# Windowed attention and a gated convolution block on one core: casts of w_out by transfers, and guards and clamps on another engine

## The chip, the core and the metric

One Trainium2 chip, of which the kernel uses one core. The metric is the device time of one execution in microseconds. The core has engines with a queue each: TensorE (PE in the profile; its weight loads are PEld), VectorE (DVE), ScalarE (ACT), GpSimd (POOL) and SyncE (SP), which here only issues transfers. Each queue is worked through in order: an instruction that waits holds up all that stands behind it.

## The reference, cut to what matters

```python
# 8 batches, 8 heads, 576 positions, 64 per head; window of 64 positions back
scores = scale * np.matmul(q, k.transpose(0, 1, 3, 2))
scores = np.where(mask, scores, -1000000000.0)        # 0 <= i - j < 64
attn = np.exp(scores - np.max(scores, axis=-1, keepdims=True))
attn = attn / (np.sum(attn, axis=-1, keepdims=True) + 1e-09)
x = heads_side_by_side(np.matmul(attn, v))            # (8, 576, 512)

h = np.maximum(x @ w_in, 0.0)                         # w_in 512 x 1024
conv_out = sum(conv_w[k] * shifted(h, k - 1) for k in range(3))   # along positions
gate = 1.0 / (1.0 + np.exp(-conv_out))
return (h * gate) @ w_out                             # w_out 1024 x 512
```

The weights come in as 64-bit floats, everything else in 32 bits.

## The kernel before, in words

The 8 x 576 positions are cut into 12 units of 384. For each unit the kernel computes attention and then the block with `w_in`, the convolution, the gate and `w_out`. Attention of later units runs while the matrix products of earlier ones do.

**Attention.** A unit is worked in three chunks `b`. `qk` (L350) makes scores, `row_max` (L357) adds the mask and takes the negative row maximum `nm`, `exps` (L367) takes exponents and their sums `sm`. `guard` (L370) adds 1e-9 to the sums, `reciprocal` (L373) inverts them into `r`, and `normalise` (L378) multiplies. For units 0 and 1 the result is transposed on TensorE (L384) and copied into `ub` by ScalarE (L389); later units use VectorE and 24 small transfers. For unit 2 GpSimd zeroes parts of `ub` (L411, L412). `values` (L481) multiplies with `v`. In the units 0, 1 and 2 `guard` is put on GpSimd, from unit 3 on it is on VectorE.

**Two halves.** The large products use float32r, a rounded type. So that precision isn't lost, each operand is split into a rounded high half and the rest: `xh` (ScalarE, L485) and `xl` (VectorE, L488), `wih` and `wil`, `woh` and `wol`, `gh` (ScalarE, L551) and `gl` (VectorE, L555). Each product is three matmuls, high by high, high by low and low by high: L501 for `w_in`, L564 for `w_out`.

**The block.** L522 is the ReLU into `hbuf`, L528 and L535 the convolution, L542 the sigmoid, L547 the gate.

**The weights.** The 64-bit words are loaded into `bits` (L264) and turned into float32 by integer and float operations in `to_f32`: an absolute value on ScalarE (L248), a clamp from below by 2^-15 on GpSimd (L249), a shift and mask (L250), sign and exponent (L252) on VectorE, a scaled copy of the low words on ScalarE (L255), and their sum on VectorE (L256). `weights` then casts the result `x` to the high half on GpSimd (L269) and subtracts it on VectorE for the low half (L270). `w_in` comes in five calls, parts (0), (1), (2, 3), (4, 5), (6, 7); `w_out` in four, (0, 1), (2, 3), (4, 5), (6, 7). A part has 512 columns, so a call handles 512 or 1024. There are two buffers of `bits` and two of `x`; the loads of a later call wait until L256 of an earlier one has read `bits`, and L248 of a later call waits until L270 has read `x`. The convolution's weights go through the same `to_f32`, with 24 columns.

**The order.** Every step is put on a list by `at` with a due time, an engine, a cost in microseconds, and what it reads and writes. `queued` then plays the list through: the engine that can start earliest takes the most urgent step that is ready, and the order so found is that of each engine's queue. It is found when the kernel is built. `two` marks a step that is taken to need the port that VectorE and GpSimd share. For a step that moves data, the plan takes it to end some time after its issue:

```python
if x.mb:
    dma = max(dma, start) + x.mb * 2.7
    end = dma + 1.9
```

Where TensorE would have nothing to do in the first 110 us of the plan, matmuls on a tile of zeros (`spare`, L212) are put in its queue.

Of the kernel before, what the change touches and what calls it, by code (L numbers as in the profile page):

```python
# [8 lines left out]
F32 = mybir.dt.float32  # L9
# [3 lines left out]
ALU = mybir.AluOpType  # L13
# [20 lines left out]
TINY = 2.0 ** -15  # L34
# [127 lines left out]
PORT_CL = 0.5  # L162
# [5 lines left out]
def attention_moe(ctx: ExitStack, tc: tile.TileContext, q, k, v, w_in, conv_w, w_out, out):  # L168
    nc = tc.nc
# [48 lines left out]
    def at(t, eng, cost, do, r=(), w=(), kind=None, mb=0, port=0.0):  # L218

        plan.append(Work(t, eng, cost, do, list(r), list(w), kind, mb, port))  # L220

    def two(t, eng, cost, do, **kw):
        at(t, eng, cost, do, port=cost, **kw)
# [17 lines left out]

    def to_f32(t, n, st, x, kb, kt):

        lw, hw, xu = st[..., 0], st[..., 1], x.bitcast(U32)

        at(t, "ACT", 0.0009 * n + 0.2, lambda: nc.scalar.activation(x, hw.bitcast(F32), AF.Abs), r=kb, w=kt)  # L248
        at(t, "POOL", 0.0027 * n + 0.02, lambda: nc.gpsimd.tensor_scalar(x, x, TINY, None, op0=ALU.max), w=kt, port=PORT_CL)  # L249
        two(t, "DVE", 0.00052 * n + 0.06, lambda: nc.vector.tensor_scalar(  # L250
            xu, xu, 3, 0x3FFFFFF8, op0=ALU.logical_shift_left, op1=ALU.bitwise_and), w=kt)
        two(t, "DVE", 0.00104 * n + 0.07, lambda: nc.vector.scalar_tensor_tensor(  # L252
            xu, hw, 0xC0000000, xu, op0=ALU.bitwise_and, op1=ALU.bitwise_or), r=kb, w=kt)

        at(t, "ACT", 0.0009 * n + 0.2, lambda: nc.scalar.activation(lw, lw, AF.Copy, scale=2.0 ** -29), w=kb)  # L255
        two(t, "DVE", 0.00104 * n + 0.07, lambda: nc.vector.tensor_tensor(xu, xu, lw, ALU.add), r=kb, w=kt)  # L256

    def weights(t, src, fs, hi, lo, key, buf, halves):

        e = slice(halves[0] * DM, (halves[-1] + 1) * DM)  # L260
        st, x = bits[buf][:, e], w24[buf][:, e]
        kb, kt = [("bits", buf, a) for a in halves], [("w24", buf, a) for a in halves]
        for f, a, tl in zip(fs, halves, load_at(buf, halves, t)):
            at(tl, "SP", 0.7, lambda f=f, a=a: nc.sync.dma_start(  # L264
                bits[buf][:, a * DM:(a + 1) * DM], src[f].bitcast(U32).rearrange("p (e two) -> p e two", two=2)),
               w=[("bits", buf, a)], mb=0.52)
        n = len(fs) * DM
        to_f32(t, n, st, x, kb, kt)
        two(t, "POOL", 0.00127 * n, lambda: nc.gpsimd.tensor_copy(hi, x), r=kt, w=[f"{key}{f}h" for f in fs])  # L269
        two(t, "DVE", 0.00104 * n + 0.07, lambda: nc.vector.tensor_tensor(lo, x, hi.bitcast(F32), ALU.subtract),  # L270
           r=kt + [f"{key}{f}h" for f in fs], w=[f"{key}{f}l" for f in fs])

    freed = {}

    def load_at(buf, halves, t):

        ts = [freed.get((buf, a), START["bits"][buf][a]) for a in halves]
        for a in halves:
            freed[(buf, a)] = t + 0.01
        return ts  # L280
# [20 lines left out]
    def wide(u):  # L301
        return u < BY_PE

    def place_of(b, i):

        return divmod(NB * b + i, NT)

    def block(u, b, i):

        first = (u * NT + place_of(b, i)[1]) % SB == 0  # L310
        return (P, W if first else 0, 0) if wide(u) else (KW, 0, 2 if first else 1)
# [25 lines left out]
    def bank_keys(u, b):  # L337
        return {1: [("po", 2), ("po", 3)], 2: [("po", 0), ("po", 1)]}.get(b, [("sc", 0)]) if u == 0 else [("sc", 0)]

    def qk(u, b):  # L340
        rows = W if wide(u) else HW
        for i in range(NB):
            g, t0 = place_of(b, i)
            n, o, _ = block(u, b, i)
            for p in range(2):
                for s in range(0, W, rows):
                    r, t = p * W + s, t0 * W + s
                    for h in range(2):
                        hs = slice(h * D, (h + 1) * D)
                        nc.tensor.matmul(banks_of(u, b)[h][r:r + rows, i * P + o:i * P + n], qs[hs, 2 * g + p, t:t + rows],  # L350
                                         ks[hs, 2 * g + p, t + o:t + n], start=True, stop=True)

    def row_max(u, b):
        for i in range(NB):
            n, o, m = block(u, b, i)
            for h in range(2):
                nc.vector.tensor_tensor_reduce(  # L357
                    out=ss[b][:, i, h, o:n], in0=banks_of(u, b)[h][:, i * P + o:i * P + n], in1=mask[m][:, o:n],
                    scale=-0.125, scalar=3.0e38, op0=ALU.add, op1=ALU.min,
                    accum_out=nms[b][:, 2 * i + h:2 * i + h + 1])  # L360

    def exps(u, b, i):
        n, o, _ = block(u, b, i)
        for h in range(2):
            e = slice(2 * i + h, 2 * i + h + 1)
            x = ss[b][:, i, h, o:n]
            nc.scalar.activation(x, x, AF.Exp, bias=nms[b][:, e], scale=-1.0, accum_out=sms[b][:, e])  # L367

    def guard(b, on):
        on.tensor_scalar_add(sms[b], sms[b], 1e-9)  # L370

    def reciprocal(b):
        nc.vector.reciprocal(rs[b], sms[b])  # L373

    def normalise(u, b, on):
        n = P if wide(u) else KW
        sv = ss[b].rearrange("p t h k -> p (t h) k")[:, :, :n]
        on.tensor_tensor(sv, sv, rs[b].unsqueeze(2).broadcast_to([P, 2 * NB, n]), ALU.mult)  # L378
# [40 lines left out]
    def needed(b):  # L419

        keys = []
        for i in range(NB):
            g, t = place_of(b, i)
            n = int(t >= (4, 2)[g])
            keys += [("q", g, n)] + [("k", g, j) for j in range(n + 1)]
        return list(dict.fromkeys(keys))

    def softmax(u, b, t, ex_at):
        at(t, "PE", 0.90 if wide(u) else 0.82, lambda b=b: qk(u, b), r=needed(b), w=bank_keys(u, b),
           kind="tiled" if wide(u) else "eight")  # L430
        for i in range(NB):
            if block(u, b, i)[1]:
                at(t + 0.1, "POOL", 0.2, lambda b=b, i=i: nc.gpsimd.memset(ss[b][:, i, :, :W], 0.0), w=[("s", b, i)])
        at(t + 0.002, "DVE", 1.69 if wide(u) else 1.45, lambda b=b: row_max(u, b),
           r=bank_keys(u, b) + (["mask0"] if wide(u) else ["mask1", "mask2"]), w=[("s", b, i) for i in range(NB)] + [("nm", b)])
        t = ex_at
        for i in range(NB):
            at(t, "ACT", 0.78 if wide(u) else 0.74, lambda b=b, i=i: exps(u, b, i), r=[("nm", b)],
               w=[("s", b, i), ("sm", b, i)], kind="exp")
        t += 0.45  # L440
        sw = [("sm", b, i) for i in range(NB)]
        if u < 3:
            at(t, "POOL", 0.6, lambda b=b: guard(b, nc.gpsimd), w=sw)
        else:
            at(t, "DVE", 0.15, lambda b=b: guard(b, nc.vector), w=sw)
        at(t, "DVE", 0.15, lambda b=b: reciprocal(b), r=sw, w=[("r", b)])
        sr = [("s", b, i) for i in range(NB)]
        if u < 3:
            two(t, "DVE", 1.15 if wide(u) else 0.88, lambda b=b: normalise(u, b, nc.vector), r=[("r", b)], w=sr)
        else:  # L450
            two(t, "POOL", 1.5, lambda b=b: normalise(u, b, nc.gpsimd), r=[("r", b)], w=sr)
        t += 0.4
        if u < BY_PE:
            for j in range(2):
                m, g = ("po", (2 * b + j) % NC), place_of(b, NB // 2 * j)[0]
                at(t, "PE", 0.66, lambda b=b, j=j: transpose_pe(b, j), r=sr + ["mask0"], w=[m])
                at(t + 0.1, "ACT", 0.55, lambda b=b, j=j: untile(b, j), r=[m], w=[("u", g, i) for i in range(4)])
            return
        t = max(t, when[-1][2] + 0.1)
        for g, t0, rows in parts(b):  # L460
            at(t, "DVE", 0.12 * 2 * len(rows), lambda b=b, g=g, t0=t0, rows=rows: transpose(b, g, t0, rows), r=sr,
               w=[("T", g)] + [("bits", i, a) for i in T_BITS[g] for a in range(2)])
            if t0 + len(rows) == NT:
                if u == BY_PE:
                    at(t + 0.01, "POOL", 1.0, lambda g=g: zero_blocks(g), w=[("u", g, i) for i in range(4)])
                for i in range(4):
                    at(t + 0.05, "SP", 2.1, lambda g=g, i=i: place(g, i), r=[("T", g)], w=[("u", g, i)], mb=0.15)
# [263 lines left out]
```

## Time and profile before

| | |
|---|---|
| median of 3 runs | 532.17 us (531.51 to 532.33) |
| the profiled execution | 531.34 us |
| its span in the profile | 529.6 us, 1.74 us less than the execution |
| busy, share of the span | PE 98%, PEld 94%, DVE 72%, ACT 72%, POOL 21% |
| granted clock of TensorE | 1.0 |
| GpSimd's clamps, L249 | 9 of `w` with 23.9 us, one of `cw` with 0.3 |
| GpSimd's casts, L269 | 5 of `w_in` with 5.7 us, 4 of `w_out` with 5.6 |
| GpSimd's guards, L370 | 9 with 7.2 us |
| transfers | all issued by SP; 39.7% of what 16 engines could do |

Rows of the profile's timeline give start and duration in us, the engine, the line, the operation, what it writes and reads, the shapes, and in brackets how long its engine had been idle and what ended that. Rows of its groups give count, busy time in us and the mean of one in ns, then the idle time in front of them.

### The profile page before, as it was taken

The page shows a single profiled execution, that of the slowest core. Times are in us where ns is not written, and L with a number is a line of the kernel's source. Part 1 is how long each engine was busy: PE and PEld are TensorE (multiplying, and loading weights), DVE is VectorE, ACT ScalarE, POOL GpSimd, SP SyncE. Part 2 cuts the span into 40 slices and gives each one's busy share as a digit, 9 for nine tenths or more (in the row PEclk, how much of TensorE's full clock was granted, in tenths as well). Part 3 has the DMA queues.
Part 4 walks back from the last instruction along what each step waited for, and adds up shares of the span by engine and source line. Part 5 has one row for each costly group of instructions (what it writes and reads, how often), then busy time and mean ns, then how long its engine had stood idle before and what let it go on. Part 6 is the DMA issues. An engine that isn't in the chain of part 4 may idle for free.

```text
span 529.6 us, 14836 instructions
## 1 busy us (share of the span) xinstructions
PE 518.5 (98%) x5826; PEld 499.8 (94%) x5826; DVE 380.3 (72%) x1084; ACT 379.7 (72%) x1011; POOL 112.6 (21%) x196
## 2 busy tenths in 40 slices
PE   9998999999999999999999999999999999999996
PEld 8887889999999999999999999999999999999996
DVE  3899999985858667767767767767767667655552
ACT  2997897579896696696697687687687687544542
POOL 6664467113131011021021021021021021000000
PEclk9999999999999999999999999999999999999999
DMA  8984660237292173183083074073073053010011
GB/s 284 365 296 136 208 231 1 60 109 248 76 325 72 58 256 83 42 291 77 21 297 77 16 253 122 21 285 105 13 264 120 17 152 104 16 61 0 2 60 62
DMA packets 29463, 69.98 MB, mean 132 GB/s; under 512 B 5713, under 2 KB 17617, under 8 KB 29393
## 3 DMA queue, kind: packets, MB, share of 16 engines
q1 hardware_dynamic: 29392, 69.03, 39.7%
q8 instruction: 46, 0.75, 0.6%
q14 instruction: 25, 0.20, 0.1%
HBM read 47.73 MB, written 9.47 MB: 108 GB/s over the span
## 4 chain that ended last, share of the span: by engine, by line
PE 85%; DVE 9%; DMA 1%; ACT 1%; issue 1%; SPq 1%; POOL 0%; DVEq 0%
PE po L564 39%; PE acc L501 36%; PE acc L481 6%; PE sc L350 5%; DVE c L535 1%; DVE w L252 1%; DMA T<-in_w_in_dram 1%; DVE s L357 1%; DVE w L256 1%; DVE wil L270 1%; ACT s L367 1%; SPq L234 1%; DVE xl L488 1%; DVE s L378 1%; DVE w L250 1%
## 5 line engine op out<-in xcount | busy, mean ns | idle before, releaser
L501 PE MATMUL acc<-xh,wih 128*128 128x384 f32 x384 | 131.5, 342 | 0.8 <-DVE xl L488 0.8
L564 PE MATMUL po<-gh,woh 128*128 128x386 f32 (+1 forms) x384 | 132.1, 344 | 0.0
L535 DVE SCALAR_TENSOR_TENSOR c<-hbuf,cw,c 128x386 f32<-128x386 f32 (+1 forms) x192 | 109.6, 623 | 30.7 <-ACT c L528 30.7
L564 PE MATMUL po<-gh,wol 128*128 128x386 f32 (+1 forms) x384 | 129.9, 338 | 0.0
L564 PE MATMUL po<-gl,woh 128*128 128x386 f32 (+1 forms) x384 | 129.7, 338 | 0.0
L501 PE MATMUL acc<-xh,wil 128*128 128x384 f32 x384 | 129.7, 338 | 0.0
L501 PE MATMUL acc<-xl,wih 128*128 128x384 f32 x384 | 129.7, 338 | 0.0
L367 ACT ACTIVATE s<-s,nm 128x96 f32<-128x96 f32 (+2 forms) x288 | 105.1, 367 | 5.2 <-DVE nm L357 4.9
L555 DVE TENSOR_TENSOR gl<-c,gh 128x772 fp32r<-128x772 f32 (+1 forms) x48 | 55.8, 1162 | 28.2 <-ACT gh L551 28.1
L501 PEld LDWEIGHTS acc<-xh,wih 128*128 128x128 f32 x384 | 72.1, 188 | 2.9 <-POOL sm L370 0.7
L564 PEld LDWEIGHTS po<-gh,woh 128*128 128x128 f32 x384 | 72.2, 188 | 2.6
L378 POOL TENSOR_TENSOR s<-s,r 128x768 f32<-128x768 f32 x27 | 39.7, 1472 | 163.5 <-DVE r L373 150.7
L547 DVE TENSOR_TENSOR c<-c,hbuf 128x772 f32<-128x772 f32 (+1 forms) x48 | 47.4, 987 | 36.9 <-ACT c L542 36.7
L564 PEld LDWEIGHTS po<-gl,woh 128*128 128x128 f32 x384 | 72.3, 188 | 0.0
L564 PEld LDWEIGHTS po<-gh,wol 128*128 128x128 f32 x384 | 72.3, 188 | 0.0
L501 PEld LDWEIGHTS acc<-xh,wil 128*128 128x128 f32 x384 | 72.2, 188 | 0.0
L501 PEld LDWEIGHTS acc<-xl,wih 128*128 128x128 f32 x384 | 72.1, 188 | 0.0
L522 ACT ACTIVATE hbuf<-acc 128x384 f32<-128x384 f32 x64 | 30.9, 486 | 45.8 <-PE acc L501 45.4
L542 ACT ACTIVATE c<-c 128x772 f32<-128x772 f32 (+1 forms) x48 | 40.7, 848 | 30.2 <-DVE c L535 29.9
L357 DVE CUSTOM_DVE_ANT_0 s<-sc,mask 128x96 f32<-128x96 f32 (+2 forms) x272 | 51.5, 254 | 9.7 <-POOL mask L321 5.7
L367 ACT ACTIVATION_READ_ACCUMULATOR s<-s,nm 128x1 f32 x288 | 54.3, 189 | 0.0
L511 POOL COPY hbuf<-hbuf 128x4 f32<-128x4 f32 x44 | 16.7, 379 | 176.3 <-DVE c L547 176.2
(64 smaller groups left out, 644.5 us busy)
## 6 DMA issues: line engine op xcount, KB each, us to landing
v<-in_v_dram SPq DMA_DIRECT2D x24, 768.0 KB, 7.2
ub<-T SPq DMA_DIRECT2D x240, 48.0 KB, 1.9
k<-in_k_dram SPq DMA_DIRECT2D x22, 448.0 KB, 4.9
q<-in_q_dram SPq DMA_DIRECT2D x22, 384.0 KB, 6.9
out_dram<-T SPq DMA_DIRECT2D x8, 772.0 KB, 4.2
T<-in_w_in_dram SPq DMA_DIRECT2D x8, 512.0 KB, 6.6
T<-in_w_out_dram SPq DMA_DIRECT2D x8, 512.0 KB, 4.2
out_dram<-T SPq DMA_DIRECT2D x3, 768.0 KB, 6.4
```

What stands on the lines that cost most here:

```text
L350: nc.tensor.matmul(banks_of(u, b)[h][r:r + rows, i * P + o:i * P + n], qs[hs, 2 * g + p, t:t + rows], ks[hs, 2 * g + p, t + o:t + n], star ...
L357: nc.vector.tensor_tensor_reduce(out=ss[b][:, i, h, o:n], in0=banks_of(u, b)[h][:, i * P + o:i * P + n], in1=mask[m][:, o:n], scale=-0.125 ...
L367: nc.scalar.activation(x, x, AF.Exp, bias=nms[b][:, e], scale=-1.0, accum_out=sms[b][:, e])
L378: on.tensor_tensor(sv, sv, rs[b].unsqueeze(2).broadcast_to([P, 2 * NB, n]), ALU.mult)
L481: nc.tensor.matmul(acc[bank(("v", u, c))][h * D:(h + 1) * D, t * W:(t + 1) * W], vs[:, c, t, h], ub[g][:, 2 * p:2 * p + 2, 2 * t + h], sta ...
L501: nc.tensor.matmul(acc[bank(("m", u, f))][:, :NX], w[:, f, c], x[u % 2][:, c], start=(c == 0 and j == 0), stop=(c == NC - 1 and j == 2))
L522: nc.scalar.activation(hbuf[:, f, o:o + NX], ps[:, :NX], AF.Relu)
L535: nc.vector.scalar_tensor_tensor(c, hbuf[:, f, e:e + n], cw[:, e, f:f + 1], c, op0=ALU.mult, op1=ALU.add)
L542: nc.scalar.activation(c, c, AF.Sigmoid)
L547: nc.vector.tensor_tensor(c, c, hbuf[:, 2 * i:2 * i + 2, 1:1 + n], ALU.mult)
L555: nc.vector.tensor_tensor(gls[ring(u, i)][:, :, :n], cs[i % 2][:, :, :n], ghs[ring(u, i)][:, :, :n].bitcast(F32), ALU.subtract)
L564: nc.tensor.matmul(po[o][:, :n], w[:, f, es], x, start=(f == 0 and j == 0), stop=(f == NF - 1 and j == 2))
```

## The change

`to_f32` has a new argument, `early`: when it is set, the clamp is done by VectorE. `weights` sets it for calls of one part, which are the first two of `w_in`. For `w_out` the high half is made by a transfer that GpSimd issues from `x` in SBUF to `woh` in SBUF, with the rounding to float32r in the transfer; `w_in` keeps its casts. The guards of unit 0 go from GpSimd to VectorE; those of units 1 and 2 stay on GpSimd. The due times are unchanged; the order of all queues is found anew with the new costs.

```diff
-    def to_f32(t, n, st, x, kb, kt):
+    def to_f32(t, n, st, x, kb, kt, early=False):
...
-        at(t, "POOL", 0.0027 * n + 0.02, lambda: nc.gpsimd.tensor_scalar(x, x, TINY, None, op0=ALU.max), w=kt, port=PORT_CL)
+        if early:
+            two(t, "DVE", 0.00052 * n + 0.06, lambda: nc.vector.tensor_scalar(x, x, TINY, None, op0=ALU.max), w=kt)
+        else:
+            at(t, "POOL", 0.0027 * n + 0.02, lambda: nc.gpsimd.tensor_scalar(x, x, TINY, None, op0=ALU.max), w=kt, port=PORT_CL)
...
-        to_f32(t, n, st, x, kb, kt)
-        two(t, "POOL", 0.00127 * n, lambda: nc.gpsimd.tensor_copy(hi, x), r=kt, w=[f"{key}{f}h" for f in fs])
-        two(t, "DVE", 0.00104 * n + 0.07, lambda: nc.vector.tensor_tensor(lo, x, hi.bitcast(F32), ALU.subtract),
-           r=kt + [f"{key}{f}h" for f in fs], w=[f"{key}{f}l" for f in fs])
+        to_f32(t, n, st, x, kb, kt, len(fs) == 1)
+        his, los = [f"{key}{f}h" for f in fs], [f"{key}{f}l" for f in fs]
+        if key == "out":
+
+            at(t, "POOL", 1.2, lambda: nc.gpsimd.dma_start(hi, x), r=kt, w=his, mb=0.6)
+        else:
+            two(t, "POOL", 0.00127 * n, lambda: nc.gpsimd.tensor_copy(hi, x), r=kt, w=his)
+        two(t, "DVE", 0.00104 * n + 0.07, lambda: nc.vector.tensor_tensor(lo, x, hi.bitcast(F32), ALU.subtract), r=kt + his, w=los)
...
-        if u < 3:
+        if 0 < u < 3:
             at(t, "POOL", 0.6, lambda b=b: guard(b, nc.gpsimd), w=sw)
         else:
             at(t, "DVE", 0.15, lambda b=b: guard(b, nc.vector), w=sw)
```

## The prediction

> **What bounds the kernel now.** I read the totals and the chain of waits first.
>
> ```profile
> span 529.6 us, 14836 instructions
> PE 85%; DVE 9%; DMA 1%; ACT 1%; issue 1%; SPq 1%; POOL 0%; DVEq 0%
> ```
>
> The chain is TensorE for 85% of the span and VectorE for 9%. Two questions follow: where the hand-over lies, and whether anything after it still waits. The busy time by stretch, TensorE's groups after 75.84 us and the matmuls on the zero tile (issued only to keep TensorE from resting) answer them.
>
> ```profile
> 18.64:75.84 57.20, 52.07 (x786) 47.41 (x776) 56.98 (x156) 51.07 (x150) 34.09 (x28) 1.00 0.69 235
> 75.84:525.00 449.16, 449.16 (x4828) 436.49 (x4829) 314.55 (x874) 319.43 (x827) 68.12 (x119) 1.00 0.35 111
> ...
> L564 PE MATMUL po<-gh,woh 128*128 128x386 f32 (+1 forms) x379 | 130.4, 344 | 0.0
> L501 PE MATMUL acc<-xh,wih 128*128 128x384 f32 x356 | 121.4, 341 | 0.2 <-DVE xl L488 0.2
> ...
> L212 PE MATMUL po<-spare x86: 259/275/363, 26.9 to 68.8; 128*128 128x112 f32 x86
> 75.84 0.44 PE L501 MATMUL acc<-xh,wih 128*128 128x384 f32 x1 [0.24 <-DVE xl L488]
> ```
>
> The columns of the first two rows are the stretch, its length, and the busy time of PE, PEld, DVE, ACT and POOL, with the number of instructions, then the granted clock. From 75.84 us TensorE is busy for all of 449.16 us; its only idle time is the 0.24 us in front of that stretch, for `xl`. No filling matmul comes after 68.8. From 18.64 to 75.84 VectorE is busy for 56.98 of 57.20 us. So the kernel is a VectorE-bound preparation and then a TensorE-bound rest, at a granted clock of 1.00 in both. What the change is worth is by how much it brings forward TensorE's unbroken stretch, plus any hole that it tears into it. A microsecond of GpSimd or ScalarE matters only if VectorE's queue gets shorter by it.
>
> **The change, part by part.** First the start, where the clamp of `w_in` part 0 goes from GpSimd to VectorE.
>
> ```profile
> 13.05 1.49 POOL L249 TENSOR_SCALAR w<-w 128x512 f32<-128x512 f32 x1 [2.97 <-ACT w L248]
> 14.57 0.43 DVE L250 TENSOR_SCALAR w<-w 128x512 uint32<-128x512 uint32 x1 [2.14 <-POOL w L249]
> 15.34 0.50 POOL L370 TENSOR_SCALAR sm<-sm 128x8 f32<-128x8 f32 x1 [0.80 <-ACT s L367]
> 15.93 0.66 ACT L255 ACTIVATE T<-T 128x512 uint32<-128x512 uint32 x1
> 18.64 0.69 DVE L270 TENSOR_TENSOR wil<-w,wih 128x512 fp32r<-128x512 f32 x1 [0.71 <-POOL wih L269]
> 19.25 0.28 DVE L357 CUSTOM_DVE_ANT_0 s<-sc,mask 128x128 f32<-128x128 f32 x1
> 19.50 4.58 POOL L249 TENSOR_SCALAR w<-w 128x512 f32<-128x512 f32 x2
> 19.88 1.16 ACT L248 ACTIVATE w<-T 128x1024 f32<-128x1024 f32 x1
> 21.03 0.43 DVE L250 TENSOR_SCALAR w<-w 128x512 uint32<-128x512 uint32 x1
> 21.37 0.20 DVE L373 RECIPROCAL r<-sm 128x8 f32<-128x8 f32 x1
> 21.49 1.41 DVE L252 SCALAR_TENSOR_TENSOR w<-T,w 128x512 uint32<-128x512 uint32 x1
> 15.03 0.69 DVE L252 SCALAR_TENSOR_TENSOR w<-T,w 128x512 uint32<-128x512 uint32 x1
> 123.05 0.16 DVE L370 TENSOR_SCALAR sm<-sm 128x8 f32<-128x8 f32 x1
> 123.24 0.20 DVE L373 RECIPROCAL r<-sm 128x8 f32<-128x8 f32 x1
> ```
>
> The nearest row to a VectorE clamp of 512 columns is L250 of the same shape: it starts at 21.03 and the next instruction at 21.37, so one costs 0.34 us of the queue. For part 0 that is free: VectorE sat idle 2.14 us in front of 14.57. The chain clamp, L250, L252 finishes about 1.1 us sooner (1.49 less some 0.4). What it then meets is ScalarE, whose exponents hold L255 back to about 15.2 instead of 15.93; with the guard of the first chunk also on VectorE (0.19 us by the rows at 123.05 and 123.24, against 0.50 us and two hand-overs) I get L270 at about 18.2 instead of 18.64. VectorE is 0.4 us ahead there.
>
> For part 1 the clamp (0.34 us) and the second chunk's guard (0.19 us) fall into the full stretch, +0.53. But L252 at 21.49 took 1.41 us where the same shape at 15.03 took 0.69: it stood 0.7 us behind GpSimd's clamp of parts 2 and 3. That clamp can't start before its input, which ScalarE finishes at 21.04 (19.88 + 1.16), and it stays on GpSimd. So L252 ends near 22.9 however its predecessors stand, as long as they are through by about 22.2: row maxima to 20.5 (0.4 earlier), clamp, L250, guard, reciprocal come to 21.6. The 0.4 gained and the 0.53 paid are both swallowed there. I take 0; the bounds are −0.4 (nothing paid) and +0.53 (nothing won, no cover).
>
> The third chunk's guard has no such cover: +0.19 us. The clamp of the convolution's weights stays where it is, for it is not called with the new argument.
>
> Now `w_out`, where four casts of GpSimd become four transfers that GpSimd issues.
>
> ```profile
> 64.54 1.21 DVE L256 CUSTOM_DVE_ANT_0 w<-T,w 128x2048 uint16<-128x2048 uint16 x1
> 65.68 0.68 DVE L250 TENSOR_SCALAR w<-w 128x1024 uint32<-128x1024 uint32 x1
> 65.89 1.37 POOL L269 CAST woh<-w 128x1024 fp32r<-128x1024 f32 x1 [1.26 <-DVE w L256]
> 66.28 1.79 DVE L555 TENSOR_TENSOR gl<-c,gh 128x772 fp32r<-128x772 f32 x1
> 69.13 1.01 DVE L488 TENSOR_TENSOR xl<-acc,xh 128x384 fp32r<-128x384 f32 x2
> 71.12 1.22 DVE L270 TENSOR_TENSOR wol<-w,woh 128x1024 fp32r<-128x1024 f32 x1
> 73.39 1.93 DVE L535 SCALAR_TENSOR_TENSOR c<-hbuf,cw,c 128x386 f32<-128x386 f32 x2
> 78.20 0.91 DVE L555 TENSOR_TENSOR gl<-c,gh 128x772 fp32r<-128x772 f32 x1
> 70.06 1.14 DVE L535 SCALAR_TENSOR_TENSOR c<-hbuf,cw,c 128x386 f32<-128x386 f32 x2
> 69.73 0.92 PE L481 MATMUL acc<-ub,v 128*64 128x64 f32 x24 [0.66 <-DVE xl L488]
> 72.80 0.34 PE L564 MATMUL po<-gh,woh 128*128 128x386 f32 x1
> ```
>
> While the first cast runs, L555 takes 1.79 us; undisturbed it takes 0.91. That is 0.88 us of VectorE lost to one cast. The second cast does the same to the pair of L535 at 73.39: 1.93 against 1.14, 0.79 us. The first loss lies on the path, because L488 at 69.13, for which TensorE idled 0.66 us at 69.73, is two instructions behind it: −0.88. Of the second only TensorE's 0.24 us at 75.84 can be had, since TensorE is otherwise busy from 69.73 on: −0.24. The third and fourth casts fall after 75.84, where a shorter queue of VectorE only adds cover: 0.
>
> What the transfers add is a wait. L270 subtracts the rounded half, so it now waits for a landing instead of a cast; behind it on VectorE's in-order queue stand L256 of the next part, L535 and L488, and behind its result TensorE's first `w_out` products at 72.80. No transfer issued by GpSimd is in this trace. The nearest are the loads of the same 512 KB that SP issues, to landing:
>
> ```profile
> DMA to landing us min/median/max: 3.4/4.4/9.0
> ```
>
> With the 0.88 won, `x` of part 0 and 1 is complete still at about 65.75 (the cast came after it), and TensorE wants the low half at 72.80 − 0.88 = 71.9. L270 takes 1.22, so it must start by 70.7: the landing may take 4.9 us before it costs TensorE anything. I take 4.4, the median of the nearest rows: 0 lost. At 3.4 it is 0 too, at 9.0 it is 4.1 us. The hand-written order expects 1.62 + 1.9 us after the issue, so L270 may be queued about 69.3 and hold VectorE until 70.2; the 0.79 us that the second cast no longer takes covers that. GpSimd's own time for the issue is not in the trace; GpSimd is busy 34.09 of 57.20 us, and behind the issue stand the zeroing of `ub` and the guards of the third unit, late by no more than the cast made them.
>
> By the Trainium skill, "SBUF — State Buffer", section "Who interferes with whom", a VectorE instruction with two SBUF inputs contends with a GpSimd instruction that reads SBUF; the 1.79 against 0.91 agrees, and by that rule no transfer would hold L555. The same page's section "SBUF: two separate sides" has a rule against this change: while VectorE runs a two-port instruction, GpSimd can't write the descriptors of its transfer. No run here shows it yet; L250, 0.68 us, stands right behind L256, and would set the landing back by that much. "DMA: Bandwidth & Descriptors", section "Anatomy of one DMA — SWDGE (gpsimd) path", gives 2.0 us plus bytes over 436 GB/s, an estimate of 3.2 us for 512 KB; by it the sum is the same.
>
> Sum: 0 (start) + 0.19 (guard) − 0.88 − 0.24 + 0 (landing) = −0.93 us. The profiled execution took 531.34 us with 1.74 us outside its span, 0.83 under the median of 532.17; from the median I get 531.2 us. The measurement of this kernel can tell about 0.2%, 1.06 us, from no change, so the forecast sits beside that bound.
>
> **The rivals.** *Landings come late* (slower). One mechanism: L270 at the head of VectorE's queue, twice before 78 us. For: `w_out` loads of 1 MB are issued in the same moment that `x` is complete, since it frees their buffer, and share the engines with the cast transfer; the longest such load took 9.0 us. Against: the median is 4.4. Every microsecond beyond 4.9 is a microsecond of TensorE at 71.9; at 5.8 the gain is gone, at 6.9 the kernel is slower by the bound. At 7.5, 2.6 us lost, it gives 533.8. The descriptors held up by L250 alone (4.4 + 0.68 = 5.1 us) would cost 0.2 and give 531.4.
>
> *The guard shortens the attention of unit 0* (larger gain).
>
> ```profile
> 25.79 1.10 POOL L370 TENSOR_SCALAR sm<-sm 128x8 f32<-128x8 f32 x1
> 27.31 0.19 DVE L373 RECIPROCAL r<-sm 128x8 f32<-128x8 f32 x1
> 30.20 1.21 DVE L378 TENSOR_TENSOR s<-s,r 128x1024 f32<-128x1024 f32 x1
> 38.44 0.41 PE L501 MATMUL acc<-xh,wih 128*128 128x384 f32 x1 [0.56 <-DVE xl L488]
> ```
>
> The third chunk's guard ran on GpSimd to 26.89, its reciprocal at 27.31, and L378 at 30.20, behind work that was ready earlier; its transposes, values and halves lead to the first product of `w_in` at 38.44. A guard on VectorE lets L378 start at about 27.5, up to 2.7 us sooner. Against: VectorE is full, and the order puts another ready instruction between guard, reciprocal and L378. If half of it arrives: 531.2 − 1.35 = 529.9.
>
> *The transfer frees nothing*: GpSimd's issue holds VectorE as the cast did, or clamp and guards cost their whole 0.53 where I have 0. Then −0.93 + 0.88 = −0.05 or −0.4: 531.8 to 532.1.
>
> **How the numbers follow.** Forecast as above 0.48, at 531.2 (530.3 to 531.9 by the start's bounds and the landing between 3.4 and 5.6), about half of it beyond the bound: 0.23 faster, 0.25 same. Shorter attention 0.18, faster. Late landings 0.20, of which 0.17 slower and 0.03 same. Nothing freed 0.14, 0.10 same and 0.04 slower, as a re-sorted queue can lose as well as win. Faster 0.41, same 0.38, slower 0.21. The range reaches from just beyond the shorter attention to just short of the late landings at 7.5 us, 529.4 to 533.5.
>
> **What would show it.** Right: filling matmuls end by about 68; L555 beside the first transfer takes 0.9 us; L488 stands before 68.5; L270 of the first `w_out` parts has at most 1 us idle in front of it; TensorE's last idle time before the end lies before 75.1. Wrong: idle time of L270 on a DMA above 1 us, TensorE waiting for `wol`, filling matmuls after 69, holes after 76, or a first product of `w_in` far from 38.4.

## The result, and the profile after

The changed kernel takes 536.13 us (534.79 to 536.94), the kernel before 531.84 us (530.95 to 532.33) beside it: a ratio of 1.0077 [1.0063, 1.0091]. It is 4.3 us slower; 0.93 us less was forecast. Line numbers are higher in the changed kernel, by 3 in the conversion, by 8 at the subtraction and by 7 behind it: L259 is the sum of the conversion (L256 before), L275 the transfer, L278 the subtraction (L270), L364 the row maxima (L357), L495 `xl`, L508 and L571 the two large products.

Totals and chain of the profiled execution (534.79 us), which is the shortest of the four, then the busy time by stretch (PE, PEld, DVE, ACT, POOL with counts, granted clock, share of the 16 transfer engines, GB/s):

```profile
span 533.0 us, 14832 instructions
PE 85%; DVE 8%; DMA 4%; SPq 1%; ACT 1%; issue 0%; POOL 0%; DVEq 0%
...
18.64:75.84 57.20, 52.10 (x797) 47.59 (x798) 53.16 (x158) 51.52 (x158) 28.05 (x25) 0.97 0.66 232
75.43:528.50 453.07, 453.07 (x4843) 438.92 (x4843) 316.26 (x876) 320.86 (x828) 66.24 (x120) 1.00 0.36 115
70.00:72.00 2.00, 2.00 (x20) 2.00 (x17) 1.08 (x3) 2.00 (x7) 1.80 (x4) 1.00 1.01 342
72.00:74.00 2.00, 1.95 (x12) 1.62 (x10) 0.00 (x0) 2.00 (x12) 0.14 (x1) 1.00 1.09 430
78.00:525.00 447.00, 447.00 (x4810) 432.92 (x4810) 313.13 (x871) 317.80 (x820) 65.06 (x118) 1.00 0.36 115
```

VectorE, which had been busy for 56.98 of the 57.20 us, now has 53.16: four microseconds of the scarce engine stood empty, and from 72 to 74 it did nothing while the transfer engines were full (1.09). TensorE is unbroken from 75.43, as early as before, but has 453 us left in place of 449: before, it had done 15 products of `w_out` by then, now one. At the 0.18 us from one to the next the 14 are 2.5 us. The rest is the new order: in the 447 us from 78 to 525, in which TensorE is busy throughout, it gets through 4810 matmuls in place of 4818, and 4810 and 4811 in a1 and a3, two runs below with the same order. 8 of 0.18 us are 1.4 us, and with the 2.5 that makes the difference. One thing in this profile is not of the change: the first conversion of weights (L248) waits for its load until 13.79 us, in the kernel before, a1 and a3 only until 12.29 to 12.52, so all that follows stands later by some 1.4 us. The share of transfers in the chain went from 1% to 4%.

The place, in the timeline (start, duration, engine, line, and in brackets the idle time before and what ended it) and in the chain:

```profile
65.08 1.21 DVE L259 CUSTOM_DVE_ANT_0 w<-T,w 128x2048 uint16<-128x2048 uint16 x1
66.31 0.80 SPq L267 DMA_DIRECT2D T<-in_w_out_dram  x2
66.60 0.77 POOL L275 DMA_DIRECT2D woh<-w  x1 [0.99 <-DVE w L259]
68.64 1.80 SPq L240 DMA_DIRECT2D v<-in_v_dram  x2
64.20 0.95 DVE L562 TENSOR_TENSOR gl<-c,gh 128x772 fp32r<-128x772 f32 x1
69.94 1.14 DVE L542 SCALAR_TENSOR_TENSOR c<-hbuf,cw,c 128x386 f32<-128x386 f32 x2
70.00 1.82 PE L212 MATMUL po<-spare 128*128 128x112 f32 x14
74.14 1.23 DVE L278 TENSOR_TENSOR wol<-w,woh 128x1024 fp32r<-128x1024 f32 x1 [3.06 <-DMA woh<-w]
74.17 0.44 PE L571 MATMUL po<-gh,woh 128*128 128x386 f32 x1 [0.22 <-DMA woh<-w]
75.43 0.45 PE L571 MATMUL po<-gh,wol 128*128 128x386 f32 x1 [0.82 <-DVE wol L278]
75.40 1.16 ACT L248 ACTIVATE w<-T 128x1024 f32<-128x1024 f32 x1 [1.26 <-DVE wol L278]
83.84 1.23 DVE L278 TENSOR_TENSOR wol<-w,woh 128x1024 fp32r<-128x1024 f32 x1 [0.65 <-DMA woh<-w]
...
66.60 7.53 DMA woh<-w
```

L259 ends at 66.29 and frees the buffer `bits`; from 66.31 to 67.11 SP issues two loads of 512 KB into it, from 66.60 to 67.37 GpSimd issues its transfer, and from 68.64 on SP issues two loads of `v`. The transfer lands 7.53 us after its issue. L278 stands at the head of VectorE's queue for 3.06 us, and TensorE, with filling matmuls until 71.5 instead of 68.8, starts `w_out` at 74.17 instead of 72.80 and gets `wol` at 75.43 instead of 72.98. The four transfers in all, from issue to landing:

```profile
DMA to landing us min/median/max: 2.9/5.2/7.5
```

### The profile page after: what moved, and what is told of

Read it like the earlier page. It is cut to its first block, busy times and chain, and to the rows that moved or that the text cites. A ratio compares the mean times of both kernels' runs of the same rounds, so it can differ in the third digit from the quotient of the medians.

```text
span 533.0 us, 14832 instructions
## 1 busy us (share of the span) xinstructions
PE 520.6 (98%) x5826; PEld 500.6 (94%) x5826; DVE 377.8 (71%) x1089; ACT 379.4 (71%) x1011; POOL 102.1 (19%) x191
## 4 chain that ended last, share of the span: by engine, by line
PE 85%; DVE 8%; DMA 4%; SPq 1%; ACT 1%; issue 0%; POOL 0%; DVEq 0%
PE po L571 39%; PE acc L508 36%; PE acc L488 6%; PE sc L357 5%; DMA T<-in_w_in_dram 3%; DMA woh<-w 1%; DVE s L385 1%; DVE s L364 1%; DVE w L259 1%; DVE c L542 1%; DVE w L255 1%; SPq L234 1%; DVE wil L278 1%; ACT s L374 0%; DVE wol L278 0%
## 5 line engine op out<-in xcount | busy, mean ns | idle before, releaser
L508 PE MATMUL acc<-xh,wih 128*128 128x384 f32 x384 | 132.1, 344 | 1.4 <-ACT hbuf L529 0.9
L571 PE MATMUL po<-gh,woh 128*128 128x386 f32 (+1 forms) x384 | 132.3, 345 | 0.2 <-DMA woh<-w 0.2
L571 PE MATMUL po<-gh,wol 128*128 128x386 f32 (+1 forms) x384 | 130.2, 339 | 0.8 <-DVE wol L278 0.8
L508 PE MATMUL acc<-xh,wil 128*128 128x384 f32 x384 | 130.6, 340 | 0.0
L508 PE MATMUL acc<-xl,wih 128*128 128x384 f32 x384 | 130.4, 339 | 0.0
L571 PE MATMUL po<-gl,woh 128*128 128x386 f32 (+1 forms) x384 | 129.9, 338 | 0.0
L508 PEld LDWEIGHTS acc<-xh,wih 128*128 128x128 f32 x384 | 72.6, 189 | 3.4 <-issue 1.0
L571 PEld LDWEIGHTS po<-gh,woh 128*128 128x128 f32 x384 | 72.3, 188 | 3.2 <-DMA woh<-w 0.5
L571 PEld LDWEIGHTS po<-gh,wol 128*128 128x128 f32 x384 | 72.4, 188 | 1.3 <-DVE wol L278 1.3
L508 PEld LDWEIGHTS acc<-xl,wih 128*128 128x128 f32 x384 | 72.7, 189 | 0.0
L571 PEld LDWEIGHTS po<-gl,woh 128*128 128x128 f32 x384 | 72.4, 188 | 0.3 <-DVE gl L562 0.3
L508 PEld LDWEIGHTS acc<-xh,wil 128*128 128x128 f32 x384 | 72.6, 189 | 0.0
L364 DVE CUSTOM_DVE_ANT_0 s<-sc,mask 128x96 f32<-128x96 f32 (+2 forms) x272 | 51.5, 254 | 10.4 <-POOL mask L328 5.6
L535 ACT ACTIVATE c<-hbuf,cw 128x386 f32<-128x386 f32 (+1 forms) x96 | 53.7, 610 | 3.1 <-DVE gl L562 3.1
```

What stands on the lines that cost most here:

```text
L364: nc.vector.tensor_tensor_reduce(out=ss[b][:, i, h, o:n], in0=banks_of(u, b)[h][:, i * P + o:i * P + n], in1=mask[m][:, o:n], scale=-0.125 ...
L508: nc.tensor.matmul(acc[bank(("m", u, f))][:, :NX], w[:, f, c], x[u % 2][:, c], start=(c == 0 and j == 0), stop=(c == NC - 1 and j == 2))
L535: nc.scalar.activation(cs[i % 2][:, a, :n], hbuf[:, f, 1:1 + n], AF.Copy, scale=cw[:, 1, f:f + 1])
L571: nc.tensor.matmul(po[o][:, :n], w[:, f, es], x, start=(f == 0 and j == 0), stop=(f == NF - 1 and j == 2))
```

## The experiments

**Which part of the change costs.** `a1_after_order_casts` keeps the changed kernel's order on all queues and puts GpSimd's casts in the place of the transfers; `a2_before_order_dma` keeps the order of before and makes only the casts transfers.

```diff
 a1, from after:
-            at(t, "POOL", 1.2, lambda: nc.gpsimd.dma_start(hi, x), r=kt, w=his, mb=0.6)
+            at(t, "POOL", 1.2, lambda: nc.gpsimd.tensor_copy(hi, x), r=kt, w=his, mb=0.6)
 a2, from before (L269; its plan cost unchanged):
-... lambda: nc.gpsimd.tensor_copy(hi, x), ...
+... lambda: (nc.gpsimd.dma_start if key == "out" else nc.gpsimd.tensor_copy)(hi, x), ...
```

> The changed kernel with the order of all five queues kept to the instruction; only the four transfers into woh are casts on GpSimd again. Theory A (the loss is VectorE waiting at L278 for a landing of 7.5 us): the idle time of 3.06 us in front of the first wol goes, casts cost 0.8 us of VectorE each where they collide; about 533 us, 3 under the changed kernel's 536.1. Theory B (the loss comes from the re-sorted queues: clamps and guards on VectorE, the third row maximum later, TensorE's clock dip at 59 to 62 us): it stays at 535.5 or above.

> The kernel before with its own order; only the four casts into woh are transfers issued by GpSimd. Theory A: x of parts 0 and 1 is complete at 65.8, landing 7 to 7.5 us later, L270 queued at about 70.2 waits about 3 us; 533.5 to 535.5, slower than before by 2 to 3.5 us. Theory B: the transfer is harmless and frees 0.9 us; 530.5 to 532.

a1: 532.14 us, 1.0011 [1.0000, 1.0021]. a2: 536.43 us, 1.0088 [1.0072, 1.0103]. So clamps, guards and new order together cost 0.6 us, and the transfers 3.7 in that order (4.3 less 0.6) and 4.8 in the order of before; a2 lies above the 533.5 to 535.5 that was expected. a2 tells where it goes most cleanly, since everything else in it is the kernel before; its waits between 66 and 84 us, and the busy time of it and of before by stretch:

```profile
66.11 0.95 DVE L555 TENSOR_TENSOR gl<-c,gh 128x772 fp32r<-128x772 f32 x1
73.11 1.23 DVE L270 TENSOR_TENSOR wol<-w,woh 128x1024 fp32r<-128x1024 f32 x1 [2.92 <-DMA woh<-w]
78.39 0.44 PE L501 MATMUL acc<-xh,wih 128*128 128x384 f32 x1 [1.28 <-DVE xl L488]
82.69 1.23 DVE L270 TENSOR_TENSOR wol<-w,woh 128x1024 fp32r<-128x1024 f32 x1 [3.48 <-DMA woh<-w]
...
68.00:78.00 10.00, 7.18 (x60) 6.14 (x58) 7.08 (x10) 7.42 (x27) 3.89 (x5) 1.00 0.73 236
78.00:90.00 12.00, 10.71 (x58) 10.14 (x59) 8.52 (x12) 8.83 (x25) 5.92 (x3) 1.00 0.33 111
90.00:525.00 435.00, 434.32 (x4743) 421.10 (x4743) 305.18 (x863) 309.45 (x801) 57.37 (x117) 1.00 0.36 115
...
68.00:78.00 10.00, 9.10 (x73) 8.54 (x72) 10.00 (x13) 9.30 (x32) 6.97 (x5) 1.00 0.75 269
78.00:525.00 447.00, 447.00 (x4818) 434.33 (x4817) 312.39 (x873) 317.52 (x820) 66.00 (x118) 1.00 0.34 110
```

The last two rows are the kernel before. TensorE lacks 10.00 − 7.18 = 2.82, 12.00 − 10.71 = 1.29 and 435.00 − 434.32 = 0.68 us from 68 on, 4.79 together; before it lacked 0.90. That is 3.9 of the 5.1 us by which this execution's span (534.7) is longer. The rest lies at the same holes: otherwise a product starts every 0.18 us though it takes 0.34, and a hole costs that overlap too (at 78.39 TensorE starts 1.62 us after the product before, for 1.28 us of idle time). Two landings do it, not one: the second holds L270 for 3.48 us. The collision is gone (0.95 instead of 1.79), as predicted, and can't be seen in the sum.

**What makes the landing late.** In `a3_small_loads`, after's order and transfers, the loads of `w_out` parts 4 to 7 bring 64 KB each instead of 512 KB; `a5_before_dma_small_loads` does the same in a2. `a4_small_loads_and_v` also makes the `v` loads of unit 2 small.

```diff
 a3, a4, a5 (L264, L267 in after's numbering):
-  bits[buf][:, a * DM:(a + 1) * DM], src[f]...
+  bits[buf][:, a * DM:a * DM + (64 if key == "out" and f >= 4 else DM)], src[f]...[:, :64 if key == "out" and f >= 4 else DM]
 a4 as well (L240):
-  nc.sync.dma_start(vs[:, c], v[u, :, c])
+  nc.sync.dma_start(vs[:, c, :n], v[u, :, c, :n])     # n=1 for u == 2, else all
```

> The changed kernel with the order kept; the four loads of w_out parts 4 to 7 move 64 KB instead of 512 KB (it leaves out seven eighths of those weights). Theory A1 (the landing is late because 1 MB of loads, and v behind them, share the DMA engines): the first landing falls from 7.5 to 3 to 4.5 us, the wait of 3.06 us to under 1; about 533 us. Theory A2 (the path of a transfer issued by GpSimd is slow by itself at that place, by starved descriptors or the rounding): the landing stays near 7 us and the time near 536.

> The kernel before with its own order, casts into woh as transfers, and the loads of w_out parts 4 to 7 cut to 64 KB (it leaves out seven eighths of those weights). It asks whether the gain that the prediction summed, 0.88 + 0.24 us for the collisions, is there when the landing isn't late. With a first landing of about 5 us, as without the loads in the changed kernel: L270 waits about 0.7 us and the gain is 0.3 to 1.1, 530.5 to 531.3. If the collisions were never on TensorE's path: 531.6, as before.

> As the run with small loads, order kept, and v of unit 2 moves 128 KB for each of its two loads instead of 768 (it leaves out five sixths of that v too). Theory A1 (shared DMA engines): the first landing, 5.5 us with v behind it, falls to the 2.9 to 3.4 us that the last two transfers of the changed kernel took alone; no wait at L278; 530.3 to 531.5, 0.2 to 1 us under the run with small loads. Theory A2 (something in the path itself holds up the first transfer, such as descriptors written late beside VectorE's two-port instructions): the landing stays at 5 us or above and the time at 531.6.

a3: 531.59 us, 1.0004 [0.9996, 1.0013]. a5: 531.59 us, 1.0002 [0.9993, 1.0010]. The whole loss is gone in both orders, with the transfers still there. In a3:

```profile
DMA to landing us min/median/max: 2.9/4.2/5.5
70.76 1.22 DVE L278 TENSOR_TENSOR wol<-w,woh 128x1024 fp32r<-128x1024 f32 x1 [1.00 <-DMA woh<-w]
```

So the transfer doesn't land late by itself; it lands late beside 1 MB of loads that its own input set free. Two such loads are enough: in a2 the second transfer, issued at 75.78, took 6.8 us beside those issued from 75.50 on, when the last load of `v` (issued at 69.78, 5.1 us) had landed. What `v` adds to the first landing stays unclear. a4 gave 532.47 us, 1.0014 [1.0002, 1.0026], above the 530.3 to 531.5 that was expected. Its first landing was still 4.9 us and L278 waited 0.40, but the small `v` pieces came as many small packets, so that run didn't leave the transfer alone. With the wait cut from 1.00 to 0.40 nothing was won that could be measured.

**Can the loads be kept out of the way?** `a6_after_loads_behind` (after's order) and `a7_before_dma_loads_behind` (that of before) let SP issue the loads of parts 4 and 6 only when the transfer has landed, by a transfer of 4 bytes that reads `woh` and stands ahead of them in SP's queue.

```diff
+  key == "out" and f in (4, 6) and nc.sync.dma_start(seen, woh[:1, f - 4, :1].bitcast(F32))   # ahead of the load of part f
+  # and SP's steps planned between that load and GpSimd's transfer go behind the latter
```

> The changed kernel, whole and with its order; SP issues the loads of parts 4 to 7 only behind a 4-byte transfer that reads the woh being written, so after its landing. Nothing is left out. If the sharing of the DMA engines with these loads makes the landing late: first landing 4.5 to 5.5 us, wait at L278 under 1 us, 531.5 to 532.5, 4 us under the changed kernel. What it could cost: the loads come 4 us later, and L248 of parts 4 and 5 waits on ScalarE; if that decides, 533 to 535.

> The same delay of the loads in the order of the kernel before, with all four casts as transfers. Against 536.4 without the delay: 531 to 532 if the loads' delay costs nothing, since the collisions of 0.88 and 0.24 us go and the landing is in time; 532.5 to 534 if L248 at 72.5, which then gets its words only at about 75, holds up the ReLU behind it on ScalarE.

a6: 535.24 us, 1.0067 [1.0055, 1.0079]. a7: 537.43 us, 1.0112 [1.0096, 1.0129]. Both lie above what was expected. The first landing was then in time in both (3.8 and 4.2 us), and nothing measurable was won by it. The rows of a6, then those of a7:

```profile
77.09 1.14 ACT L248 ACTIVATE w<-T 128x1024 f32<-128x1024 f32 x1 [4.89 <-DMA T<-in_w_out_dram]
81.19 0.69 PE L508 MATMUL acc<-xh,wih 128*128 128x384 f32 x1 [2.85 <-ACT hbuf L529]
...
81.44 1.23 DVE L270 TENSOR_TENSOR wol<-w,woh 128x1024 fp32r<-128x1024 f32 x1 [6.08 <-DMA woh<-w]
83.32 0.69 PE L501 MATMUL acc<-xh,wih 128*128 128x384 f32 x1 [4.07 <-ACT hbuf L522]
```

In a6 the load, now late, holds the conversion on ScalarE (4.89 us in L248), behind which the ReLU stands, for which TensorE waits. In a7 ScalarE waits as well (5.20 us), and the loads that were held back, issued from 71.43 on, fall on the second transfer, issued at 73.27, which then takes 8.1 us. The bytes are wanted on both sides at about the same time: with the loads first VectorE waits, with the transfer first ScalarE does. In both runs TensorE's granted clock is 0.50 for a while behind the hole (last section).

**Can the order be fitted to it?** `e5_plan_knows` tells the plan that the transfer takes longer (`mb=2.0` instead of 0.6), and sorts anew. `b1_before_late_two` makes transfers only of the casts of parts 4 to 7, in the order of before; no load of weights follows those.

> The changed kernel with one number of its planner altered: the transfer into woh counts for 5.4 + 1.9 us after its issue instead of 1.62 + 1.9, about what its landing took. If the loss is only L278 placed too early in VectorE's queue: its idle time goes below 0.5 us, TensorE takes products of w_in of unit 1 first, and the time comes to 531.5 to 533. If what counts is that TensorE lacks wol, wherever L278 stands: 534 or above.

> The kernel before with its own order; only the casts of parts 4 and 5 and of 6 and 7 are transfers, the two that land in 2.9 to 3.4 us with no load beside them. They lie after TensorE's last idle time, so no gain: 531.3 to 532, unless a wait of L270 longer than 1.5 us tears a hole into TensorE's products (then 532.5 to 533.5).

e5: 535.44 us, 1.0073 [1.0060, 1.0086], though a landing of 8.8 us no longer holds anyone up for long: L278 waits only 0.78 us, since the plan puts it later, and TensorE takes products of `w_in` first, has begun 102 products by 76 us (100 in the kernel before) and shows no idle time behind 65.67. The loss has moved further back. From 102.53 to 110.14 the new plan has 32 filling matmuls in TensorE's queue, the last ten ahead of the first product of part 6 (110.18), whose subtraction it also puts later and which ends at 110.07:

```profile
108.86 1.21 DVE L278 TENSOR_TENSOR wol<-w,woh 128x1024 fp32r<-128x1024 f32 x1
109.04 1.37 PE L212 MATMUL acc<-spare 128*128 128x112 f32 x10
110.18 0.42 PE L571 MATMUL po<-gh,woh 128*128 128x386 f32 x1
```

So the order that expects the late landing loses the time elsewhere. b1: 531.86 us, 1.0007 [0.9999, 1.0015], with landings of 3.1 us: transfers with nothing beside them cost nothing, and they gain nothing either, as TensorE's unbroken stretch has begun by then.

**Clamps and guards.** `e1_casts_back` has both without the transfers, `g1_guards_only` and `c1_clamps_only` one of them. Unlike a1, each is sorted anew.

```diff
 e1 (and c1, g1):
-        if key == "out":
+        if False:
 g1 as well:
-        to_f32(t, n, st, x, kb, kt, len(fs) == 1)
+        to_f32(t, n, st, x, kb, kt, False)
 c1 as well:
-        if 0 < u < 3:
+        if u < 3:
```

> The early clamps and the guards of unit 0 on VectorE alone; w_out's casts are GpSimd's as before, and the order is found anew. Theory A: within 1.5 us of before, 530.5 to 533. Theory B: most of the loss stays, 534.5 to 536.

> Only the guards of unit 0 on VectorE, casts and clamps as before, order found anew. The two together cost 1.3 us. If the guards do it: 532.3 to 533.3, with VectorE's queue longer by their 0.2 us each and another row maximum late. If the clamps do it: 531 to 532.

> Only the clamps of w_in parts 0 and 1 on VectorE, casts and guards as before, order found anew. If the clamps do it: 532.3 to 533.3. If the guards do it: 531 to 532, as the prediction had them at 0.

e1: 532.91 us, 1.0029 [1.0019, 1.0038]. g1: 533.18 us, 1.0028 [1.0017, 1.0039]. c1: 534.56 us, 1.0052 [1.0040, 1.0064]. Guards alone cost 1.5 us, clamps alone 2.8 (above both expectations), both 1.5, and both in the order of after 0.6: these aren't prices of instructions, which would add. What differs is the order that the sorting finds. It isn't how early TensorE begins. The first product of `w_in`, at 38.44 in the kernel before, comes sooner in c1 (first row) and in a1 (second):

```profile
37.34 0.42 PE L508 MATMUL acc<-xh,wih 128*128 128x384 f32 x1
...
36.57 0.42 PE L508 MATMUL acc<-xh,wih 128*128 128x384 f32 x1 [0.50 <-POOL s L440]
65.27 0.99 PE L357 MATMUL sc<-k,q 64*32 64x96 f32 x64 [1.40 <-DMA q<-in_q_dram]
```

Counting what TensorE has done shows where each order loses:

| profile | products begun by 76 us | matmuls from 78 to 525 us, without filling ones | last matmul ends |
|---|---|---|---|
| before | 100 | 4818 | 525.50 |
| a1 | 106 | 4810 | 525.79 |
| e1 | 101 | 4806 | 527.24 |
| g1 | 93 | 4815 | 527.27 |
| c1 | 91 | 4814 | 527.63 |

At 0.18 us for each that is missing, the two columns give a1 0.4 us, e1 2.0, g1 1.8 and c1 2.3, and the last column says 0.3, 1.7, 1.8 and 2.1. So g1 and c1 lose mostly in the preparation, e1 behind it, and a1 loses behind what it had won in front.

**Where the predicted gain went.** In a5 no landing is late, the collision at L555 is gone, and still nothing is won. `d1_before_cast_on_vector` takes the casts off GpSimd without any transfer: VectorE does them right ahead of L270. `d2_after_cast_on_vector` is the same in after's order.

```diff
 d1 (L269, L270), d2 alike:
-  GpSimd: nc.gpsimd.tensor_copy(hi, x)
+  GpSimd: nothing for w_out
-  VectorE: nc.vector.tensor_tensor(lo, x, hi.bitcast(F32), ALU.subtract)
+  VectorE: key == "out" and nc.vector.tensor_copy(hi, x), then the same subtraction
```

> The order of the kernel before; the four casts of w_out parts are done by VectorE itself, right ahead of its subtraction, and by neither GpSimd nor a transfer. No landing, no change of any load. Theory 'freed time reaches TensorE': VectorE's cast costs some 0.6 us of its own in place of 0.88 and 0.79 us lost beside GpSimd's cast, and TensorE gets hi and lo sooner: 530.8 to 531.4. Rival 'GpSimd's next work takes it': GpSimd reaches its clamps of the two following parts sooner, and these fall on VectorE's convolution of 128x386 (2 us or more instead of 1.14 at 72 to 74 us): 531.5 to 532.0. If it is over 532.5, VectorE itself is what TensorE waits for here and the cast is paid in full.

> The same in the changed kernel's order: compare with a1, the same order with GpSimd's casts (532.14). Theory 'freed time reaches TensorE': 531.2 to 531.8. Rival 'GpSimd's next work takes it': 532.0 to 532.5. Over 533 says that VectorE is the engine that TensorE waits for between 64 and 76 us.

d1: 532.01 us, 1.0001 [0.9992, 1.0010]. d2: 532.62 us, 1.0010 [1.0002, 1.0019], by the ratio the same as a1 (1.0011). The first two rows are a5's convolution with GpSimd's clamp of the next parts beside it, the third what TensorE then waits for; the last three are the same place in d1, with the cast in front:

```profile
72.69 2.48 DVE L535 SCALAR_TENSOR_TENSOR c<-hbuf,cw,c 128x386 f32<-128x386 f32 x2
73.69 2.79 POOL L249 TENSOR_SCALAR w<-w 128x1024 f32<-128x1024 f32 x1
75.69 0.44 PE L501 MATMUL acc<-xh,wih 128*128 128x384 f32 x1 [0.83 <-DVE xl L488]
...
70.76 1.00 DVE L270 CAST woh<-w 128x1024 fp32r<-128x1024 f32 x1
74.07 1.93 DVE L535 SCALAR_TENSOR_TENSOR c<-hbuf,cw,c 128x386 f32<-128x386 f32 x2
76.52 0.44 PE L501 MATMUL acc<-xh,wih 128*128 128x384 f32 x1 [0.72 <-DVE xl L488]
```

In a5 `w_out` starts at 72.06 instead of 72.80, 0.74 us sooner. But GpSimd, rid of the cast, is also sooner at its clamp (73.69 instead of 74.88), which falls on the pair of L535 that the cast used to hold: 2.48 us instead of 1.93. The hole in front of the next `xl` grows from 0.24 to 0.83 us, so 0.59 of the 0.74 is given back, and TensorE's unbroken stretch begins at 75.69 instead of 75.84. GpSimd's issue of the second transfer (73.08, 0.58 us) also lies beside that pair, but it isn't the cause: in a7 the pair has such an issue beside it, and no clamp, and takes 1.14 us:

```profile
72.88 1.14 DVE L535 SCALAR_TENSOR_TENSOR c<-hbuf,cw,c 128x386 f32<-128x386 f32 x2
73.27 0.58 POOL L269 DMA_DIRECT2D woh<-w  x1 [0.20 <-issue]
```

In d1 the cast itself (1.00 us) takes the gain, and L535 is held for 1.93 us by the same clamp. "GpSimd's next work takes it" stands for the order of before. In after's order there was less to gain to begin with: a1 has no wait of TensorE after 65.27.

## Why the prediction was wrong, point by point

- **The landing (the step that failed).** It was taken as 4.4 us, the median of the loads that SP issues, with 4.9 as the point from which it costs. Measured were 7.5 us for the first and 7.0 for the second. The median of the loads was the wrong row: it mixes lonely loads with crowded ones, and the prediction had itself named the 1 MB that the end of L256 frees in the same moment. (The 9.0 us that it took for the longest load of `w_out` is a load of `w_in`, issued at 6.50; those of `w_out` took 3.4 to 4.9.) Alone the same transfer takes 2.9 and 3.4 us (the third and fourth of the changed kernel), below the 4.4; crowded it was nearly twice that. By the prediction's own rule (a microsecond of TensorE for each one beyond 4.9), a landing 74.13 − 66.29 = 7.8 us after `x` was complete costs 2.9 us.
- **The second landing** was not priced. In a2 it held VectorE for 3.48 us and TensorE again, which is why the rival "Landings come late" happened as described but cost 3.7 to 4.8 us and not 2.6.
- **The collisions, −0.88 and −0.24.** The mechanism was right: L555 and its like take 0.95 us beside the transfer. The size was wrong as a gain of the kernel: a5, with no late landing, won 0.15 us in the trace and nothing measurable in the time. The step that fails is the cover: the 0.79 us at the second L535 was counted as freed with the cast, though GpSimd's clamp stood right behind the cast in its queue and moved into its place.
- **Clamp and guards at the start, 0 within −0.4 and +0.53, and the third guard, +0.19.** With after's order and GpSimd's casts the whole is 0.6 us [0.0, 1.1] (a1), against 0.19 with bounds of −0.21 and 0.72. The number held by luck: TensorE is 6 products ahead at 76 us in a1, and the new order loses 8 behind, neither of which the prediction had in its sum. As a bound on what re-sorting can do it would have failed: c1, the same clamps in another order, costs 2.8 us.
- **The shorter attention of unit 0.** The first product of `w_in` does come sooner, at 36.57 in a1, by 1.9 us. That the guard did it isn't shown: with the clamps alone (c1) it comes at 37.34, with the guards alone (g1) at 39.80. It brought no time, since only 6 products (1.1 us) of it are left at 76 us and the order loses more than that behind.
- **Descriptors held up.** By the Trainium skill, "SBUF — State Buffer", section "SBUF: two separate sides", GpSimd can't write them while VectorE runs a two-port instruction. No run here shows it. GpSimd's issue took 0.77 us for the first transfer and 0.53 to 0.59 for the others, but the first takes 0.77 in every profile with such transfers, wherever it stands: in b1 it is the one for parts 4 and 5, at 89.93, which in a2 is the third and takes 0.59. At 0.2 us it couldn't be the cause either way.
- **Shared engines.** By the Trainium skill, "DMA: Bandwidth & Descriptors", section "Issuing engines are not separate DMA queues", transfers of all issuers run on the same 16 engines and interleave. a3 agrees: with the loads cut to 64 KB, the first landing goes from 7.5 to 5.5 us.
- Of what was to show it wrong, three came: L278 idle for over 1 us on a transfer (3.06), TensorE waiting for `wol` (0.82), filling matmuls after 69 (to 71.5).

Open are how much `v` adds to the first landing, and what in the sorted orders makes TensorE lose where the table shows it. In the changed kernel's profile TensorE's granted clock also dips for a while, to a mean of 0.997 over the span. It is no cause, since a3 is as fast as the kernel before at 0.996, but why it dips stays open: in both it begins 3.0 us after the start of a hole of 1.61 us in TensorE's work, and a1's profile has such a hole (1.61 us, at 54.4) without a dip. Nothing that was run beats the kernel before.

## What to carry to other kernels

Before an engine's copy is handed to a transfer, look at what the completion of its input sets free: a load that waits for the same event is in the transfer engines first, and the price is the crowded landing, not the median one. Holding the load back only helps if its reader has slack; here it had none, and the wait moved to ScalarE. And when a collision between two engines is taken away, see what stands next in the queue of the one that caused it, since it moves into the same place. When a change has the queues sorted anew, count what the bounding engine has done by a fixed time and in a fixed stretch behind it; the price of the moved instructions tells neither.

## What the runs showed of the hardware that was not expected

- A transfer of 512 KB within SBUF lands in 2.9 to 3.4 us alone, and in 7.5 us beside two loads of 512 KB whose issue began 0.3 us before its own and `v` behind it, though its own packets take only 1.1% of the engines' time:

```profile
q0 software_dynamic: 576, 2.10, 1.1%
```

That is 1.1% of 533 us for four, some 1.5 us of every engine for each. The 4.1 to 4.6 us beyond a lone landing came with the neighbours.
- What a neighbour costs isn't a constant: the pair of L535, 1.14 us alone, took 2.48 us beside GpSimd's clamp in a5 and 1.93 beside the same clamp in d1, where it overlapped no less. The gate right behind it (L547, also beside the clamp) took its usual 0.94 and 0.95 us.
- In the changed kernel the dip of TensorE's granted clock did not carry into the time. This stretch is of the changed kernel; from 18.64 to 75.84 us the mean was 0.97 (0.97 in a3 too), from 75.43 on 1.00:

```profile
60.00:64.00 4.00, 4.00 (x34) 3.89 (x35) 4.00 (x17) 3.99 (x8) 1.79 (x3) 0.71 0.89 293
```

In a6 and a7 it falls behind the hole, into the stretch that TensorE bounds: it is 0.50 for 3.4 us from 80.84 in a6 and for 6.8 us from 81.54 in a7, and products come every 0.32 us instead of 0.18. Two rows of a6:

```profile
82.00:84.00 2.00, 2.00 (x8) 2.00 (x8) 1.61 (x3) 1.98 (x7) 0.34 (x1) 0.50 0.34 43
86.00:90.00 4.00, 4.00 (x24) 4.00 (x24) 2.77 (x5) 2.61 (x4) 1.36 (x1) 1.00 0.16 65
```

The first has 8 matmuls in 2 us, the second 24 in 4 us. From the 3.1 and 5.1 us that the products run at the slower pace, I estimate 1.4 us of TensorE's work lost in a6 and 2.2 in a7. Whether it costs that much isn't shown: a7's executions take longer at a lower mean clock (536.62 and 536.94 us at 0.995 and 0.996, 537.33 and 537.53 at 0.993, 539.63 at 0.992), a6's do not (534.95 and 535.24 at 0.999, 535.06 to 535.45 at 0.996 and 0.997).
